# Attention scores in two row halves of the matrix array instead of one product with block-diagonal keys

## The chip, the cores and the metric

The kernel runs on one NeuronCore of one Trainium2 chip. The core has TensorE (PE in the profile; its weight loads are listed apart as PEld), VectorE (DVE), ScalarE (ACT), GpSimd (POOL) and SyncE (SP, which here only issues DMAs). The metric is the device time of one execution in microseconds (us); lower is better.

## What is computed

Attention with keys and values averaged in groups of 8, then two feed-forward layers over the 4608 tokens that come out of it. The part around the change is the first function:

```python
def _attn_ref(q, k, v):                      # each 8 x 8 x 576 x 64: batch, head, token, feature
    B, H, S, D = q.shape
    pool = 8
    Sp = S // pool                           # 72 averaged keys
    scale = 1.0 / np.sqrt(D)
    k_p = k.reshape(B, H, Sp, pool, D).mean(axis=3)
    v_p = v.reshape(B, H, Sp, pool, D).mean(axis=3)
    scores = scale * np.matmul(q, k_p.transpose(0, 1, 3, 2))
    scores = scores - np.max(scores, axis=-1, keepdims=True)
    attn = np.exp(scores)
    attn = attn / (np.sum(attn, axis=-1, keepdims=True) + 1e-09)
    return np.matmul(attn, v_p)

def reference(**kwargs):                     # attn, then 512 -> 2048 -> 512, then 512 -> 1536 -> 512
    x = attn_out.transpose(0, 2, 1, 3).reshape(B * S, H * D)
    x = _moe_ref(x=x, **moe_kwargs)          # g(x @ w_in) @ w_out, g a rational function
    return _moe2_ref(x=x, **moe2_kwargs)     # (sigmoid(x @ w_gate) * (x @ w_val)) @ w_out
```

All of it is in fp32. A head has 64 features, so the sum that makes one score runs over 64 of the array's 128 rows.

## The kernel before

**Tiles and stages.** The tokens are cut into 36 tiles of 128 (`units`). A batch has 576 tokens, four and a half tiles, so four of the tiles hold the end of one batch and the start of the next ("parts"); with them there are 40 parts of a tile. Four tiles make a block of 512 tokens. For each block the attention gives the operand `xs`, and the first feed-forward layer takes 16 steps: `g1` (products into `h`, lines 628 to 630 by the helper `mm3`), the rational function on ACT, DVE and POOL, and `g2` (products into `acc`, the same lines). The attention of a block is woven into the steps of the block before it. The second feed-forward layer has no attention beside it and takes the second half of the time.

**Scores of one part (`tile_attention`, from line 550).** The queries of a tile stand as `raw`: 128 partitions by four groups `j` of 128 tokens, where partitions 0 to 63 hold the features of head 2j and 64 to 127 those of head 2j+1. The averaged keys `kp` have the same two halves. `place_keys` (line 470) copies them, once in a batch, with four ACT instructions (line 476) into `kbd`, a block-diagonal tile that line 733 fills with zeros at the start: the copies put the even head's 72 keys beside zeros in the upper half, the odd head's in the lower half. One matmul (line 569) with a 128-row stationary operand (the queries) and 144 moving columns of `kbd` then gives the scores of two heads. Two such matmuls fill a PSUM bank `sc` with four neighbouring heads, so a part has two PE tasks, each with a bank of its own. DVE takes the maximum (574) and subtracts it (575), ACT the exponential (578), DVE the sum and its reciprocal (583, 584), and POOL the product (586). PE transposes the result (594, `pta`), ACT evacuates it (596, `aT`), and PE multiplies with the averaged values (610, `psx`).

That last product shows in the trace what a divided array does: an even head writes PSUM partitions 0 to 63 and an odd head 64 to 127, so its matmuls run in the two column halves of the array (tile shape "72\*64" in the profile).

**What sets the order.** All tasks up to the last block are handed to a planner (`Planner`, line 49): each has an engine, an estimated cost and a rank, and claims named buffers. The planner runs through estimated time and writes out one fixed order for each engine; the engines then run theirs in that order and wait on semaphores. There are four PSUM banks for `h`, `sc`, `pta` and `psx` beyond the first block, at most three of them for attention and at most three for `h`.

Of the kernel before, what the change touches and what calls it, by code (L numbers as in the profile page):

```python
# [13 lines left out]
AF = mybir.ActivationFunctionType  # L14
ALU = mybir.AluOpType
AX = mybir.AxisListType
# [172 lines left out]
def attention_moe_glu_kernel(ctx: ExitStack, tc: tile.TileContext, q, k, v, w_in, w_out, ca, cb, w_gate, w_val, w_out2, out):  # L189
    nc = tc.nc  # L190

    B, H, S, D = v.shape
# [3 lines left out]
    P = 128  # L196
    POOL = 8
    SP = S // POOL
    NJ = H // 2
# [17 lines left out]
    wp = ctx.enter_context(tc.tile_pool(name="wp", bufs=1))  # L217
# [15 lines left out]
    slots = {"W": [f"w{i}" for i in range(NF1 + FS + NR)], "ST": [f"st{i}" for i in range(6)],  # L233
             "h": [f"b{i}" for i in range(4)], "su": [f"su{i}" for i in range(3)], "y": [f"y{i}" for i in range(3)],
             "m": [f"m{i}" for i in range(3)], "g": [f"g{i}" for i in range(3)], "xs": ["xs0", "xs1"],
             "raw": [f"raw{i}" for i in range(3)], "e": ["e"], "aT": ["aT"], "kp": ["kp"], "vp": ["vp"],
             "vh": ["vh0", "vh1"], "kbd": ["kbd"]}
    slots.update({f"acc{e}": [f"b{4 + e}"] for e in range(NJ)})
    slots.update({n: [n] for n in ("mx0", "mx1", "r0", "r1", "wqt")})
    for n in ("A11", "S2", "S3", "S1", "A12", "A22", "S4"):  # L240
# [4 lines left out]
    pools = {}  # L245
# [204 lines left out]
    def small(shape, name, where, kind=None):  # L450
        return Buf(name, shape, F32, where, kind)

    kbd = small([P, NJ, 2, SP], "kbd", ["kbd"])
    vh, xs, rawq, turned, pooled = {}, {}, {}, [], {}

    def k_cols(c):
# [2 lines left out]
    def keys(b, rank, rank_load):  # L459
# [6 lines left out]
            plan("DVE", dve(m * POOL), rank, lambda raw=raw, m=m, cols=cols: nc.vector.reduce_sum(  # L466
                kp.t[:, cols], raw.t[:, :m * POOL].rearrange("p (s j) -> p s j", j=POOL), axis=AX.X), w=[(kp, c)], r=[raw])
        pooled[b] = kp

    def place_keys(b, rank):  # L470
        kp = pooled.pop(b)
        for js, cs in ((slice(0, NJ // 2), (0, 1, 2)), (slice(NJ // 2, NJ), (2, 3, 4))):
            for e in range(2):
                half = slice(e * D, (e + 1) * D)
                def fn(e=e, js=js, half=half):
                    nc.scalar.activation(kbd.t[half, js, e], kp.t.rearrange("p (j s) -> p j s", s=SP)[half, js], AF.Copy)
                plan("ACT", act(SP * 2), rank, fn,
                    w=[(kbd, (js.start, e))], r=[(kp, c) for c in cs])

    def values0(rank, rank_load):  # L480
        vp = small([P, NCH, D], "vp", ["vp"])
# [68 lines left out]
    def tile_attention(i, rank, gate_on=[]):  # L550
# [8 lines left out]

        for x, (b, n) in enumerate(parts):  # L560
            rows = slice(x * n, (x + 1) * n)
            if i == first[b]:
                place_keys(b, rank)
            for g in range(2):
                sc = psum("sc", own, kind)

                def fn(g=g, sc=sc):
                    for j in (2 * g, 2 * g + 1):
                        nc.tensor.matmul(sc.t[:, (j % 2) * 2 * SP:(j % 2 + 1) * 2 * SP], raw.t[:, j * P:(j + 1) * P], kbd.t[:, j].rearrange("p e s -> p (e s)"), start=True, stop=True)  # L569
                plan("PE", 0.5, rank, fn, w=[sc], r=[raw, (kbd, (2 * g, 0)), (kbd, (2 * g, 1))],  # L570
                     after=(turned[-1:] if blk > 1 else turned[-3:-2]) + gate_on)
                hs = slice(4 * g, 4 * g + 4)
                scv = lambda sc=sc, rows=rows: sc.t[rows, :4 * SP].rearrange("p (h s) -> p h s", s=SP)
                plan("DVE", dve(288) - 0.04, rank, lambda hs=hs, scv=scv, rows=rows: nc.vector.reduce_max(mx.t[rows, hs], scv(), axis=AX.X), w=[(mx, (g, x))], r=[sc])
                plan("DVE", dve(288) - 0.04, rank, lambda hs=hs, scv=scv, rows=rows, n=n: nc.vector.tensor_tensor(
                    out=e_.t[rows, hs, :SP], in0=scv(), in1=mx.t[rows, hs].unsqueeze(2).to_broadcast([n, 4, SP]), op=ALU.subtract),
                    w=[(e_, (g, x))], r=[sc, (mx, (g, x))])
        plan("ACT", act(576), rank, lambda: nc.scalar.activation(e_.t[:, :, :SP], e_.t[:, :, :SP], AF.Exp, scale=scale / POOL),
             w=[(e_, (g, x)) for g in range(2) for x in range(len(parts))])
        r = small([P, H], "r", [f"r{i % 2}"])  # L580
# [148 lines left out]

    T0 = -20.0  # L730
    values_at = {}
    for c in range(1):
        plan("DVE", 0.6, T0, lambda: nc.vector.memset(kbd.t, 0.0), w=[kbd])
    warm = psum("warm", ["acc2"])

    def fn():
        for x in range(12):
            nc.tensor.matmul(warm.t[:, :P], ident, ident, start=True, stop=True)
# [52 lines left out]
    for n in range(N1):  # L791
        i, f = SEQ[n]
        emit_extra(n + 2)
        if n >= SEG and f >= FS:
            wo_stream(f, n - 1.5)
        if n == 3 * SEG + 1:
            half_load(n)
        x = n - last_step
        if x == BX:
            bar = plan("-", 0.0, n, "late", after=[t for t in plan.tasks if any(b.where and b.where[0] in  # L800
                       ("ST", "raw", "e", "aT", "kp", "vp", "vh", "kbd", "mx0", "mx1", "r0", "r1") for b in t.bufs)])
            rawx[0] = Buf("rawx", [P, 8 * TB], F32, ["xs"])
            for h, d, ib, o, m in x_pieces(0):
                load(n, 4 * m / 2, lambda h=h, d=d, ib=ib, o=o, m=m: nc.sync.dma_start(x_dst(h, d, m), x2d[ib].t[:, :, o:o + m]),
                     w=[(rawx[0], (h, d))], r=[x2d[ib]], after=first_mm[-1:])
        if 1 <= x <= NQ:
            t = x - 1
            ring[t] = w_buf("wq")
            src, o = ring_src(t)
            load(n, 512, lambda t=t, src=src, o=o: nc.sync.dma_start(ring[t].t.bitcast(F32), src.t[:, o:o + 2]), w=[ring[t]], r=[src], after=first_mm[-1:])  # L810
        if BX + 3 <= x <= BX + 6:
            for job in X_PREP[x - BX - 3]:
                if job[0] == "split":
# [16 lines left out]
    with tc.manual_schedule():  # L830
# [4 lines left out]
        sm = att.enter_context(tc.tile_pool(name="sm", bufs=1))  # L835
        stage = att.enter_context(tc.tile_pool(name="stage", bufs=1))
        stage_t.append(stage.tile([P, len(slots["ST"]) * 8 * P], F32, name="stage"))
        pools.update(w=wp, b=ps, su=rot, y=rot, m=rot, g=g_p, xs=xs_p, raw=raw_p, e=ap1, aT=ap1, kp=ap1, vp=ap1, vh=ap1, kbd=ap1,
                     mx=sm, r=sm)
        for t in jobs:  # L840
            if t.fn == "late":
# [358 lines left out]
```

## Time and profile before

| what | value |
|---|---|
| median of 3 runs | 1736.67 us (1735.71 to 1737.2) |
| the profiled execution, its own time | 1734.64 us |
| its span, first to last instruction | 1732.6 us |
| mean granted TensorE clock | 0.996 of full speed |
| TensorE busy | 1709.0 us, 99% of the span |
| ScalarE, VectorE, GpSimd busy | 60%, 71%, 42% |

The span is cut into four stretches below: 0 to 32 us (the first block's attention alone), 32 to 110 us (weights come in and are split while the first steps run), 110 to 830 us (steps with attention woven in) and 830 us to the end (no attention). A matmul in fp32 is two records in the profile, each with its weight load; "x8" of line 569 is four matmuls. The durations that the profile gives matmuls overlap, so a cost on PE is read from starts: of the matmul ahead of a group and of the second one after it.

### The profile page before, as it was taken

What the parts mean: (1) busy time and instruction counts of PE and PEld (TensorE: products, weight loads), DVE (VectorE), ACT (ScalarE), POOL (GpSimd) and SP (SyncE); (2) the same over time, 40 slices, a digit from 0 to 9 for tenths busy, and PEclk for the clock granted to TensorE, in tenths of its full rate; (3) what the DMA queues carried; (4) which work ended last, traced back from release to release, by engine and by line L of the source; (5) the groups of instructions that cost most, each with busy time, mean ns of one, the idle gap of its engine ahead of it and who ended that gap; (6) DMA issues with size and microseconds to landing.
All of it is one profiled execution on the core that took longest, in us unless ns stands there. A gap on an engine that the chain in (4) does not pass through costs nothing.

```text
span 1732.6 us, 28635 instructions
## 1 busy us (share of the span) xinstructions
PE 1709.0 (99%) x10044; PEld 1553.5 (90%) x10044; DVE 1235.0 (71%) x2146; ACT 1046.6 (60%) x1957; POOL 730.0 (42%) x807
## 2 busy tenths in 40 slices
PE   7899999999999999999999999999999999999999
PEld 6688888888888888788889999999999999999999
DVE  7898888888887878788786466466466467457456
ACT  6999778787877878898885244244244234235234
POOL 6675356454644646777544320330330330330320
PEclk9999999999999999999999999999999999999999
DMA  7675463545535446775753998888888888888856
GB/s 242 190 278 197 158 192 127 177 145 181 187 116 184 146 157 187 227 239 185 235 181 120 301 317 279 277 265 279 272 272 280 277 265 279 272 270 279 255 181 207
DMA packets 180867, 384.61 MB, mean 222 GB/s; under 512 B 24692, under 2 KB 92276, under 8 KB 180724
## 3 DMA queue, kind: packets, MB, share of 16 engines
q1 hardware_dynamic: 180724, 382.78, 67.4%
q8 instruction: 80, 1.31, 0.3%
q14 instruction: 63, 0.52, 0.1%
HBM read 322.96 MB, written 58.72 MB: 220 GB/s over the span
## 4 chain that ended last, share of the span: by engine, by line
PE 93%; ACT 2%; DMA 1%; DVE 1%; POOL 1%; issue 0%; SPq 0%; POOLq 0%; ACTq 0%
PE h L628 17%; PE h L630 17%; PE h L629 17%; PE acc L628 7%; PE acc L630 7%; PE acc L629 7%; PE acc L1044 5%; PE acc L1043 5%; PE acc L1042 5%; PE sc L569 2%; PE psx L610 2%; PE pta L594 2%; DMA stage<-in_moe_w_in_dram 0%; ACT stage L296 0%; DMA rawv<-in_v_dram 0%
## 5 line engine op out<-in xcount | busy, mean ns | idle before, releaser
L933 DVE TENSOR_TENSOR t<-h,t 128x384 f32<-128x384 f32 x360 | 200.8, 558 | 251.2 <-PE h L630 123.0
L668 POOL TENSOR_TENSOR g<-y,g 128x512 fp32r<-128x512 f32 x143 | 186.6, 1305 | 205.3 <-ACT g L666 175.7
L1002 POOL TENSOR_TENSOR ga<-t 128x384 f32<-128x384 f32 x48 | 48.9, 1019 | 452.5 <-DVE t L933 445.6
L628 PE MATMUL h<-xs,wi 128*128 128x512 f32 x576 | 228.9, 397 | 5.7 <-ACT aT L596 3.6
L628 PE MATMUL acc<-g,wo 128*128 128x512 f32 x576 | 230.1, 399 | 0.0
L630 PE MATMUL acc<-g,wo 128*128 128x512 f32 x576 | 225.2, 391 | 1.9 <-POOL g L668 1.9
L630 PE MATMUL h<-xs,wi 128*128 128x512 f32 x576 | 225.3, 391 | 0.0
L629 PE MATMUL h<-xs,wi 128*128 128x512 f32 x576 | 225.2, 391 | 0.0
L629 PE MATMUL acc<-g,wo 128*128 128x512 f32 x576 | 224.6, 390 | 0.0
L1044 PE MATMUL acc<-wo,go 128*128 128x256 f32 x756 | 213.9, 283 | 0.0
L1043 PE MATMUL acc<-wo,go 128*128 128x256 f32 x756 | 213.9, 283 | 0.0
L1042 PE MATMUL acc<-wo,go 128*128 128x256 f32 x756 | 213.9, 283 | 0.0
L628 PE MATMUL h<-xS,wq 128*128 128x384 f32 x576 | 192.4, 334 | 0.0
L630 PE MATMUL h<-xS,wq 128*128 128x384 f32 x576 | 192.4, 334 | 0.0
L629 PE MATMUL h<-xS,wq 128*128 128x384 f32 x576 | 192.4, 334 | 0.0
L947 ACT ACTIVATE t<-h 128x384 f32<-128x384 f32 x72 | 35.3, 491 | 242.2 <-PE h L630 238.4
L662 DVE SCALAR_TENSOR_TENSOR y<-y,coef,h 128x512 f32<-128x512 f32 x144 | 107.2, 744 | 70.9 <-ACT h L661 70.5
L1044 PEld LDWEIGHTS acc<-wo,go 128*128 128x128 f32 x756 | 145.1, 192 | 0.0
L1043 PEld LDWEIGHTS acc<-wo,go 128*128 128x128 f32 x756 | 145.1, 192 | 0.0
L1042 PEld LDWEIGHTS acc<-wo,go 128*128 128x128 f32 x756 | 145.1, 192 | 0.0
L628 PE MATMUL h<-xA,wq 128*128 128x384 f32 x432 | 144.3, 334 | 0.0
L629 PE MATMUL h<-xA,wq 128*128 128x384 f32 x432 | 144.3, 334 | 0.0
(129 smaller groups left out, 4258.1 us busy)
## 6 DMA issues: line engine op xcount, KB each, us to landing
wq<-w2d SPq DMA_DIRECT2D x252, 512.0 KB
wo<-wo2d SPq DMA_DIRECT2D x126, 512.0 KB
wo<-wod SPq DMA_DIRECT2D x96, 512.0 KB
w2d<-stage SPq DMA_DIRECT2D x36, 512.0 KB
wo2d<-stage SPq DMA_DIRECT2D x84, 128.0 KB
rawk<-in_k_dram SPq DMA_DIRECT2D x32, 256.0 KB
rawq<-in_q_dram SPq DMA_DIRECT2D x32, 256.0 KB
rawv<-in_v_dram SPq DMA_DIRECT2D x32, 256.0 KB
```

Source lines behind the costliest of these rows:

```text
L569: nc.tensor.matmul(sc.t[:, (j % 2) * 2 * SP:(j % 2 + 1) * 2 * SP], raw.t[:, j * P:(j + 1) * P], kbd.t[:, j].rearrange("p e s -> p (e s)"), ...
L628: nc.tensor.matmul(out_, wl, xh, start=start, stop=False, skip_group_check=on)
L629: nc.tensor.matmul(out_, wh, xh, start=False, stop=False, skip_group_check=on)
L630: nc.tensor.matmul(out_, wh, xl, start=False, stop=stop, skip_group_check=on)
L662: plan("DVE", 0.66, rank, lambda: STT(out=y.t, in0=y.t, scalar=coef[:, 0:1], in1=h.t, op0=ALU.add, op1=ALU.mult), w=[y], r=[h])
L668: plan(on, cost, rank, lambda: eng.tensor_tensor(out=g.t[:, 1], in0=y.t, in1=g.t[:, 0].bitcast(F32), op=ALU.subtract), w=[(g, 1)], r=[y, ( ...
L933: nc.vector.tensor_tensor(out=out_, in0=a, in1=b, op=ALU.add)
L947: nc.scalar.activation(t["u"], b[1], AF.Copy)
L1002: eng.tensor_tensor(out=dst, in0=x, in1=y, op=ALU.mult)
L1042: nc.tensor.matmul(a, gh, wh, start=s_ == 0 and not on, stop=False, skip_group_check=on)
L1043: nc.tensor.matmul(a, gh, wl, start=False, stop=False, skip_group_check=on)
L1044: nc.tensor.matmul(a, gl, wh, start=False, stop=s_ == NS - 1, skip_group_check=on)
```

## The change

The block-diagonal tile goes away: its zeroing, its four copies in a batch, and its buffer. The scores of each head become a matmul of their own with a 64-row stationary operand, 128 token columns wide, and 72 moving columns of `kp`. Even heads use rows 0 to 63 of the array and write one bank, odd heads use rows 64 to 127 and write another. A part thus has one PE task of eight matmuls instead of two tasks of two, and claims both banks at once; the planner's cost for it is 0.6 instead of twice 0.5. DVE's two passes over a bank now take heads 0, 2, 4, 6 and heads 1, 3, 5, 7. `kp` gets a second buffer, since matmuls now read it where copies did.

```diff
-             "raw": ..., "e": ["e"], "aT": ["aT"], "kp": ["kp"], "vp": ["vp"],
-             "vh": ["vh0", "vh1"], "kbd": ["kbd"]}
+             "raw": ..., "e": ["e"], "aT": ["aT"], "kp": ["kp0", "kp1"], "vp": ["vp"],
+             "vh": ["vh0", "vh1"]}
...
-    def place_keys(b, rank):
-        kp = pooled.pop(b)
-        for js, cs in ((slice(0, NJ // 2), (0, 1, 2)), (slice(NJ // 2, NJ), (2, 3, 4))):
-            for e in range(2):
-                half = slice(e * D, (e + 1) * D)
-                def fn(e=e, js=js, half=half):
-                    nc.scalar.activation(kbd.t[half, js, e], kp.t.rearrange("p (j s) -> p j s", s=SP)[half, js], AF.Copy)
-                plan("ACT", act(SP * 2), rank, fn, w=[(kbd, (js.start, e))], r=[(kp, c) for c in cs])
...
-            if i == first[b]:
-                place_keys(b, rank)
+            sc = [psum("sc", own, kind) for _ in range(2)]
+
+            def fn(b=b, sc=sc):
+                for j in range(NJ):
+                    for g in range(2):
+                        nc.tensor.matmul(sc[g].t[:, j * SP:(j + 1) * SP], raw.t[g * D:(g + 1) * D, j * P:(j + 1) * P],
+                                         pooled[b].t[g * D:(g + 1) * D, j * SP:(j + 1) * SP], start=True, stop=True)
+            plan("PE", 0.6, rank, fn, w=sc, r=[raw, pooled[b]],
+                 after=(turned[-1:] if blk > 1 else turned[-3:-2]) + gate_on)
             for g in range(2):
-                sc = psum("sc", own, kind)
-
-                def fn(g=g, sc=sc):
-                    for j in (2 * g, 2 * g + 1):
-                        nc.tensor.matmul(sc.t[:, (j % 2) * 2 * SP:(j % 2 + 1) * 2 * SP], raw.t[:, j * P:(j + 1) * P],
-                                         kbd.t[:, j].rearrange("p e s -> p (e s)"), start=True, stop=True)
-                plan("PE", 0.5, rank, fn, w=[sc], r=[raw, (kbd, (2 * g, 0)), (kbd, (2 * g, 1))], ...)
-                hs = slice(4 * g, 4 * g + 4)
+                hs = slice(g, H, 2)
...
-        plan("DVE", 0.6, T0, lambda: nc.vector.memset(kbd.t, 0.0), w=[kbd])
```

New costs and buffers make the planner write another order. Three places matter below.

PE beyond 110 us, at one part's scores (`sc`) between steps of the first layer; the kernel before, a row being one instruction or a run of equal ones:

```order
L629 MATMUL h<-xs,wi_1318 128x512
L630 MATMUL h<-xs,wi_1318 128x512
L569 MATMUL sc<-kbd,rawq 128x144 x4
L628 MATMUL acc_2126<-g,wo_1934 128x512
L629 MATMUL acc_2126<-g,wo_1934 128x512
```

The changed kernel, where the helper's lines are 617 to 619 and the score's is 556:

```order
L618 MATMUL acc_1333<-g,wo_1909 128x512
L619 MATMUL acc_1333<-g,wo_1909 128x512
L556 MATMUL sc<-kp,rawq 128x72 x8
L617 MATMUL h<-xs,wi_1359 128x512
L618 MATMUL h<-xs,wi_1359 128x512
```

Four matmuls of 144 columns became eight of 72, between neighbours that stay matmuls of the whole array. Beyond 110 us there are 31 such parts in both orders, each alone between whole-array matmuls of 512 columns; before, three of the 31 are split into two pieces with other work between them.

SP about 40 us into the program, where the fourth piece of `w_in` (for `stage`) is issued among the copies that spread pooled values (`vh`); the kernel before:

```order
L534 DMA vh<-vp 72x64
L534 DMA vh<-vp 8x64
L534 DMA vh<-vp 64x64
L324 DMA stage<-in_moe_w_in_dram 128x4x256
L544 DMA rawq<-in_q_dram 128x512 x2
```

The changed kernel:

```order
L523 DMA vh<-vp 72x64
L324 DMA stage<-in_moe_w_in_dram 128x4x256
L523 DMA vh<-vp 8x64
L523 DMA vh<-vp 64x64
L533 DMA rawq<-in_q_dram 128x512
```

The weight load moved ahead of the last two of those copies.

ACT about 32 us into the program, at the key copies for the second batch; the kernel before:

```order
L308 ACTIVATE wi1_448<-stage_125 128x512
L296 ACTIVATE stage_125<-stage_125 128x512
L619 ACTIVATE xs_379<-psx_437 128x4x128
L298 ACTIVATE stage_125<-stage_125 128x512
L476 ACTIVATE kbd_126<-kp_331 64x2x72 x4
```

The changed kernel:

```order
L298 ACTIVATE stage_125<-stage_125 128x512
L608 ACTIVATE xs_394<-psx_441 128x4x128
L308 ACTIVATE wi1_460<-stage_125 128x512
L296 ACTIVATE stage_125<-stage_125 128x512
L298 ACTIVATE stage_125<-stage_125 128x512
```

The four copies are gone; ACT goes from one weight piece (`wi1`) to the next conversion (296, 298).

## Rows read from the trace of the kernel before

**Rows 1.** The page's busy times, and its chain that ended last by engine.
```profile
PE 1709.0 (99%) x10044; PEld 1553.5 (90%) x10044; DVE 1235.0 (71%) x2146; ACT 1046.6 (60%) x1957; POOL 730.0 (42%) x807
...
PE 93%; ACT 2%; DMA 1%; DVE 1%; POOL 1%; issue 0%; SPq 0%; POOLq 0%; ACTq 0%
```

**Rows 2.** Busy time by stretch: from:to, length, engines (instructions), granted clock, DMA, GB/s.
```profile
0.00:32.00 32.00, 23.93 (x185) 20.81 (x186) 22.82 (x46) 18.02 (x35) 18.38 (x44) 0.89 0.85 275
32.00:110.00 78.00, 68.26 (x375) 54.91 (x374) 71.02 (x119) 72.01 (x128) 58.55 (x60) 0.96 0.63 205
110.00:830.00 720.00, 717.45 (x3743) 596.38 (x3742) 594.76 (x985) 586.43 (x1052) 410.26 (x487) 1.00 0.54 179
830.00:1732.60 902.60, 899.36 (x5747) 881.41 (x5745) 546.44 (x1000) 370.09 (x746) 242.82 (x219) 1.00 0.78 256
```

**Rows 3.** The score matmuls (line 569) by stretch: PE, PEld, clock, DMA share, GB/s.
```profile
0.00:32.00 32.00, 7.95 (x40) 7.07 (x40) 0.89 0.85 275
32.00:110.00 78.00, 4.70 (x34) 4.44 (x32) 0.96 0.63 205
110.00:830.00 720.00, 35.88 (x248) 34.83 (x248) 1.00 0.54 179
```

**Rows 4.** Timeline of PE: start us, us, instruction; twelve undisturbed steps, then one part's scores.
```profile
87.18 0.39 PE L628 MATMUL acc<-g,wo 128*128 128x512 f32 x1
...
89.90 0.39 PE L628 MATMUL h<-xs,wi 128*128 128x512 f32 x1
...
243.96 0.39 PE L630 MATMUL acc<-g,wo 128*128 128x512 f32 x1
244.19 1.14 PE L569 MATMUL sc<-kbd,rawq 128*128 128x144 f32 x8
...
245.41 0.40 PE L629 MATMUL h<-xs,wi 128*128 128x512 f32 x1
```

**Rows 5.** Timeline of PE at two products with the values, of one and two tiles.
```profile
79.44 0.40 PE L630 MATMUL acc<-g,wo 128*128 128x512 f32 x1
79.77 1.09 PE L610 MATMUL psx<-aT,vh 72*64 72x128 f32 x16
...
81.13 0.39 PE L629 MATMUL acc<-g,wo 128*128 128x512 f32 x1
...
373.92 0.40 PE L630 MATMUL acc<-g,wo 128*128 128x512 f32 x1
...
376.48 0.39 PE L629 MATMUL acc<-g,wo 128*128 128x512 f32 x1
```

**Rows 6.** Weight loads by shape, whole span: busy us, mean ns, idle us before them.
```profile
L630 PEld LDWEIGHTS acc<-g,wo 128*128 128x128 f32 x576 | 108.1, 188 | 26.1 <-POOL g L668 3.3
L610 PEld LDWEIGHTS psx<-aT,vh 72*64 72x64 f32 x384 | 19.1, 137 | 8.1 <-issue 4.7 <-ACT aT L596 1.3 <-ACT h L661 1.1
```

**Rows 7.** Timeline of PEld in the selection of the first batch's values, and its last two loads.
```profile
20.11 0.54 PEld L511 LDWEIGHTS vps<-vp,sel 128*72 128x72 f32 x7
...
21.28 0.41 PEld L511 LDWEIGHTS vps<-vp,sel 128*72 128x72 f32 x3
...
L511 PEld LDWEIGHTS vps<-vp,sel x2: 136/138/139, 21.5 to 21.6; 64*72 64x72 f32 x2
```

**Rows 8.** Timeline of ACT at the four key copies of the second batch.
```profile
31.80 1.33 ACT L476 ACTIVATE kbd<-kp 64x144 f32<-64x144 f32 x4
```

**Rows 9.** Around 40 us: timelines of SP, ACT and PE, and the stretch with the clock.
```profile
37.19 2.09 SPq L534 DMA_DIRECT2D vh<-vp  x3
39.32 0.58 SPq L324 DMA_DIRECT2D stage<-in_moe_w_in_dram  x1
...
43.32 0.67 ACT L296 ACTIVATE stage<-stage 128x512 f32<-128x512 f32 x1 [1.37 <-DMA stage<-in_moe_w_in_dram]
...
45.06 0.80 PE L628 MATMUL h<-xs,wi 128*128 128x512 f32 x1 [2.65 <-ACT aT L596]
...
43.00:50.00 7.00, 4.94 (x12) 3.80 (x12) 5.99 (x11) 6.03 (x11) 2.69 (x3) 0.51 1.02 347
```

More of the change, by code (lines that the diff above doesn't have):

```diff
@@ L235, in attention_moe_glu_kernel @@
              "m": [f"m{i}" for i in range(3)], "g": [f"g{i}" for i in range(3)], "xs": ["xs0", "xs1"],
-             "raw": [f"raw{i}" for i in range(3)], "e": ["e"], "aT": ["aT"], "kp": ["kp"], "vp": ["vp"],
-             "vh": ["vh0", "vh1"], "kbd": ["kbd"]}
+             "raw": [f"raw{i}" for i in range(3)], "e": ["e"], "aT": ["aT"], "kp": ["kp0", "kp1"], "vp": ["vp"],
+             "vh": ["vh0", "vh1"]}
     slots.update({f"acc{e}": [f"b{4 + e}"] for e in range(NJ)})
@@ L451, in small @@
         return Buf(name, shape, F32, where, kind)
-    kbd = small([P, NJ, 2, SP], "kbd", ["kbd"])
     vh, xs, rawq, turned, pooled = {}, {}, {}, [], {}
@@ L468, in keys @@
         pooled[b] = kp
-    def place_keys(b, rank):
-        kp = pooled.pop(b)
-        for js, cs in ((slice(0, NJ // 2), (0, 1, 2)), (slice(NJ // 2, NJ), (2, 3, 4))):
-            for e in range(2):
-                half = slice(e * D, (e + 1) * D)
-                def fn(e=e, js=js, half=half):
-                    nc.scalar.activation(kbd.t[half, js, e], kp.t.rearrange("p (j s) -> p j s", s=SP)[half, js], AF.Copy)
-                plan("ACT", act(SP * 2), rank, fn,
-                    w=[(kbd, (js.start, e))], r=[(kp, c) for c in cs])
     def values0(rank, rank_load):
@@ L561, in tile_attention @@
             rows = slice(x * n, (x + 1) * n)
-            if i == first[b]:
-                place_keys(b, rank)
-            for g in range(2):
-                sc = psum("sc", own, kind)
-                def fn(g=g, sc=sc):
-                    for j in (2 * g, 2 * g + 1):
-                        nc.tensor.matmul(sc.t[:, (j % 2) * 2 * SP:(j % 2 + 1) * 2 * SP], raw.t[:, j * P:(j + 1) * P], kbd.t[:, j].rearrange("p e s -> p (e s)"), start=True, stop=True)
-                plan("PE", 0.5, rank, fn, w=[sc], r=[raw, (kbd, (2 * g, 0)), (kbd, (2 * g, 1))],
-                     after=(turned[-1:] if blk > 1 else turned[-3:-2]) + gate_on)
-                hs = slice(4 * g, 4 * g + 4)
-                scv = lambda sc=sc, rows=rows: sc.t[rows, :4 * SP].rearrange("p (h s) -> p h s", s=SP)
-                plan("DVE", dve(288) - 0.04, rank, lambda hs=hs, scv=scv, rows=rows: nc.vector.reduce_max(mx.t[rows, hs], scv(), axis=AX.X), w=[(mx, (g, x))], r=[sc])
+            sc = [psum("sc", own, kind) for _ in range(2)]
[6 more added lines that the diff above has]
+                 after=(turned[-1:] if blk > 1 else turned[-3:-2]) + gate_on)
+            for g in range(2):
+                hs = slice(g, H, 2)
+                scv = lambda sc=sc[g], rows=rows: sc.t[rows, :4 * SP].rearrange("p (h s) -> p h s", s=SP)
+                plan("DVE", dve(288) - 0.04, rank, lambda hs=hs, scv=scv, rows=rows: nc.vector.reduce_max(mx.t[rows, hs], scv(), axis=AX.X), w=[(mx, (g, x))], r=[sc[g]])
                 plan("DVE", dve(288) - 0.04, rank, lambda hs=hs, scv=scv, rows=rows, n=n: nc.vector.tensor_tensor(
                     out=e_.t[rows, hs, :SP], in0=scv(), in1=mx.t[rows, hs].unsqueeze(2).to_broadcast([n, 4, SP]), op=ALU.subtract),
-                    w=[(e_, (g, x))], r=[sc, (mx, (g, x))])
+                    w=[(e_, (g, x))], r=[sc[g], (mx, (g, x))])
         plan("ACT", act(576), rank, lambda: nc.scalar.activation(e_.t[:, :, :SP], e_.t[:, :, :SP], AF.Exp, scale=scale / POOL),
@@ L731, in attention_moe_glu_kernel @@
     values_at = {}
-    for c in range(1):
-        plan("DVE", 0.6, T0, lambda: nc.vector.memset(kbd.t, 0.0), w=[kbd])
     warm = psum("warm", ["acc2"])
@@ L800, in attention_moe_glu_kernel @@
             bar = plan("-", 0.0, n, "late", after=[t for t in plan.tasks if any(b.where and b.where[0] in
-                       ("ST", "raw", "e", "aT", "kp", "vp", "vh", "kbd", "mx0", "mx1", "r0", "r1") for b in t.bufs)])
+                       ("ST", "raw", "e", "aT", "kp", "vp", "vh", "mx0", "mx1", "r0", "r1") for b in t.bufs)])
             rawx[0] = Buf("rawx", [P, 8 * TB], F32, ["xs"])
@@ L837, in attention_moe_glu_kernel @@
         stage_t.append(stage.tile([P, len(slots["ST"]) * 8 * P], F32, name="stage"))
-        pools.update(w=wp, b=ps, su=rot, y=rot, m=rot, g=g_p, xs=xs_p, raw=raw_p, e=ap1, aT=ap1, kp=ap1, vp=ap1, vh=ap1, kbd=ap1,
+        pools.update(w=wp, b=ps, su=rot, y=rot, m=rot, g=g_p, xs=xs_p, raw=raw_p, e=ap1, aT=ap1, kp=ap1, vp=ap1, vh=ap1,
                      mx=sm, r=sm)
```

## The prediction

> **What bounds the kernel now.** I read the busy times first [rows 1]: PE is busy for 99% of the span and makes 93% of the chain that ended last; the next engine, DVE, stands at 71%. A share over the whole span hides stages, so the stretches come next [rows 2]. PE is idle for 32 - 23.93 = 8.1 us in the first 32 us, for 78 - 68.26 = 9.7 us from 32 to 110 us, for 720 - 717.45 = 2.6 us from there to 830 us and for 3.2 us after. So from 110 us on every nanosecond that PE gains or loses is paid out in full, while DVE (594.76 of 720 us) and ACT (586.43) have about a sixth of that time free. Before 110 us the kernel is held by loads, conversions and waits: from 32 to 110 us ACT and DVE are busy for 72 and 71 of 78 us.
>
> The changed line falls in both regions. The score matmuls show 248 records beyond 110 us [rows 3], eight to a part: 31 parts where PE is the limit. The other nine parts (40 in all) lie in the early stretches.
>
> **What a part's scores cost now.** Whole-array matmuls of 512 columns follow each other at (89.90 - 87.18) / 12 = 0.227 us [rows 4]. Around a part's scores the last of them ahead starts at 243.96 us and the second one behind at 245.41. Without the group two steps would lie between, so 0.454 us go off: 1.45 - 0.454 = 0.99 us. That is 0.124 us for each of eight records, with nothing lost at the group's ends.
>
> **What it will cost: the switch of the array.** The trace holds one kind of work that runs in halves already, the products with the values. One tile of them takes 81.13 - 79.44 - 0.454 = 1.24 us, two take 376.48 - 373.92 - 0.454 = 2.11 us [rows 5]. The second tile thus adds 0.87 us for its 16 records, 0.109 us a pair, and 1.24 - 0.87 = 0.37 us is left over: that is what entering and leaving the halves costs, once for each group. It is no oddity of column halves: at the end of the value selection two matmuls use 64 rows, and around them the loads lag too. Seven loads ahead follow each other at (0.54 - 0.145) / 6 = 0.066 us (0.145 us being the length of one). The row of three loads covers the last whole-height load and the two 64-row ones: its third starts at 21.28 + 0.41 - 0.14 = 21.55 us, two steps in 0.27 us where 0.13 would do [rows 7]. So entering a row half costs 0.14 us; the price of leaving one stands in no row by itself, and I take the 0.37 us for both. The bounds are 0 and 0.4 us. The Trainium skill's page "TensorEngine Tiling (Array Packing)", Key Properties, says that changing the tiling mode drains TensorE; both places of the trace agree.
>
> **What it will cost: the pairs.** Eight matmuls of two records make eight pairs, if an even head runs in the upper rows while an odd one runs in the lower. The column halves do that: 128 moving columns at the score's rate of 0.124 us for 144 would take 0.110 us for each record, and a pair took 0.109. What sets a pair's step here? The moving side shrinks to 72 columns, 0.062 us. The weight load doesn't: the stationary operand still has 128 token columns, on 64 rows instead of 128. Loads of 128 columns last 188 ns, those of 64 columns 137 [rows 6], 0.8 ns a column, so some 0.102 us of a 128-column load grow with its width. In the value selection loads of 72 columns beside only 64 moving ones ran at steps of 0.066 us [rows 7], longer than the 0.055 us for the moving side: there the load sets the step. Scaled from 72 to 128 columns that is between 0.110 (0.8 ns for each further column) and 0.117 us (in proportion). I take 0.112. The least is 0.109, a column pair's step; the most for parallel halves is the 0.124 of today's records. So a part takes 8 x 0.112 + 0.37 = 1.27 us in place of 0.99: 0.28 us more.
>
> The Trainium skill's page "TensorE: Matmul & The Clock Gate", LDWEIGHTS, states the rule that speaks against this change: a load's time follows its columns, whatever the number of rows. By its formula, columns over 1.2, an estimate of a 128-column load is 107 ns, and the part would come out at 8 x 0.107 + 0.37 = 1.23 us; the 188 and 137 ns agree with its slope.
>
> Beyond 110 us: 31 x 0.28 = **+8.6 us**, all of it on the path. With 0.109 and 0.32 us for the switch it would be 31 x 0.2 = 6, with 0.124 and 0.4 it would be 31 x 0.4 = 12.
>
> **The other parts of the change.** The key copies go: four in each of 8 batches, 1.33 us a batch, 10 us of ACT [rows 8]. Beyond 110 us they lie under PE and are worth nothing. The second batch's four, at 31.8 us, stand in the queue of an engine that is nearly full until 110 us, so up to 1.3 us comes back there. The first batch's stand ahead of the first scores, which now wait for the reductions alone. The zeroing on DVE runs before the first keys are in: nothing. DVE's passes keep their number and size.
>
> The order moves the fourth piece of `w_in` ahead of two copies of pooled values on SP. Three such copies take 2.09 us, so it is issued 1.4 us sooner. In the trace it was issued at 39.32 us, ACT's conversion waited for it until 43.32, an evacuation queued behind that, and the matmul at 45.06 us waited 2.65 us; from 43 to 50 us the granted clock was 0.51 of full speed, so mostly at the lower of its two levels (1.2 of 2.4 GHz), with PE idle for long before and in that stretch (4.94 us busy of 7) [rows 9]. A shorter wait gains 1.4 us, and up to 12 x 0.2 = 2.4 us if the clock stays up for the twelve matmuls of that stretch.
>
> Against that, a part now waits for two free banks at once, and DVE can start on the first only when the whole group is nearly done, 0.5 us later than now. Behind it on PE's queue stand the first layer's matmuls; who waits is the maximum, then the exponential, then the transposes. From 110 us on at least 24 whole-array matmuls (5.4 us) stand in the new order between a part's scores and its transposes, so I cost this at nothing there; without that cover it would be 31 x 0.5 = 15 us. The nine early parts pay up to 9 x 0.28 = 2.5 us. Early balance: -1.3 - 1.4 - 0.5 and then + 1.7 for the parts that don't find a wait to hide in: -1.5 us, with -6 and +3 as ends.
>
> **Sum:** +8.6 - 1.5 = +7.1 us. The profiled execution took 1734.64 us, which becomes 1741.7; it lies 2.0 us below the median of 1736.67, so the median goes to **1743.8 us**. Faster or slower by 0.2% (3.5 us) is about what a measurement of this kernel can tell from no change.
>
> **The rivals.**
> (a) *The halves' weight loads follow one another.* Nothing in the trace shows two loads in the two row halves; the column halves' loads do overlap, which speaks against it. Then 16 x 0.112 + 0.37 = 2.16 us a part, 31 x 1.17 = +36 us, and about 1771 us.
> (b) *The other side, the halves run at the moving rate.* If a load hides wholly, a pair takes 0.062 us and a part 8 x 0.062 + 0.37 = 0.87 us: 31 x -0.12 = -3.7, with the early -1.5 about 1731.5 us, faster. It decides from a step below 0.078 us, where a part costs what it does now. The 0.066 us of 72-column loads speaks against it. The Trainium skill's tiling page, Theoretical Speedup, promises up to 2x where a contraction is 64 or less; this is that rule.
> (c) *The switch is free for row halves.* 8 x 0.112 + 0.02 = 0.92 us, 31 x -0.07 = -2.2, with the early stretch 1733 us, on the line between the same and faster. The 0.14 us of [rows 7] speaks against it.
> (d) *The early stretch gives its full 6 us.* +8.6 - 6 = +2.6: 1739.3 us, within 0.2%. For it: 17.8 us of idle PE there; against it: every queue there is full, so one shortened wait mostly uncovers the next.
>
> **How the numbers follow.** Forecast 61%, (a) 13%, (b) 6%, (c) 7%, (d) 13%. The forecast's own range is 1739 to 1751 us; of its 61, some 7 fall below +3.5 us. Slower: 54 + 13 = 67, and 1 of (d): 0.68. Same: 7 + 12 + 3 of (c) = 0.22. Faster: 6 + 4 = 0.10. The range leaves out (a) and (b), 19%, and reaches down to (c): 1732 to 1752.
>
> **What would show it.** Right: the score line with 640 records, its starts in pairs some 0.11 us apart, PE groups of 1.2 to 1.35 us between whole-array matmuls, and beyond 110 us no new wait of PE. Pairs at 0.06 mean (b), single records at 0.11 mean (a), no gap at the ends means (c). The forecast is wrong if new waits on `sc` banks or on DVE's maximum show up on PE, or if the stretch before 110 us ends more than 3 us sooner or later than I put it.

## The result and the profile after

The change makes the kernel slower: 1747.22 us median (1745.50 to 1750.43, six runs) against 1736.40 (1735.13 to 1737.39, six runs) of the kernel before, a ratio of 1.0063 [1.0050, 1.0076]. Run once more on another chip it came to 1748.62 us against 1734.44, 1.0088 [1.0071, 1.0105]. The forecast was 1743.8 us, slower, with a range of 1732 to 1752. So the way was right and the time lies inside the range, and the change costs 11 to 14 us where 7 were forecast. The profiled execution took 1746.89 us, with a span of 1745.1.

The page's busy times and its chain by engine, which answer to [rows 1]:

```profile
PE 1723.7 (99%) x10364; PEld 1554.3 (89%) x10364; DVE 1234.2 (71%) x2145; ACT 1038.0 (59%) x1925; POOL 729.4 (42%) x807
...
PE 90%; ACT 3%; DVE 2%; DMA 2%; POOL 1%; issue 1%; SPq 0%; POOLq 0%; ACTq 0%
```

PE has 320 records more and is 14.7 us longer busy; ACT has lost the 32 key copies and 8.6 us. The chain gives a first hint that longer matmuls are not all of it: 3% of the span went from PE to ACT, DVE and DMA.

The stretches, as in [rows 2] (from:to, length, busy time and instructions of PE, PEld, DVE, ACT, POOL, granted clock, DMA, GB/s):

```profile
0.00:32.00 32.00, 23.95 (x211) 21.42 (x212) 20.66 (x44) 15.94 (x29) 16.94 (x42) 0.79 0.84 274
32.00:110.00 78.00, 72.98 (x422) 58.63 (x422) 64.94 (x116) 70.44 (x121) 57.12 (x61) 0.91 0.61 199
110.00:830.00 720.00, 715.57 (x3942) 583.72 (x3941) 592.72 (x975) 572.98 (x1015) 405.12 (x479) 1.00 0.53 176
```

Beyond 110 us PE is idle for 4.4 us where it was 2.6. In the two early stretches the granted clock is lower than before, 0.79 and 0.91 of full speed in place of 0.89 and 0.96.

The new score line has its 640 matmul records, each with its load. The loads (columns: count, shortest/median/longest ns, first and last start in us, shapes):

```profile
L556 PEld LDWEIGHTS sc<-kp,rawq x640: 182/188/334, 7.5 to 815.4; 64*128 64x128 f32 x160
```

A load of 64 rows and 128 columns takes 188 ns, as long as a load of 128 rows and 128 columns [rows 6]: halving the rows did not shorten it.

PE's timeline around one part (start us, us, instruction, records), to be read as [rows 4] was:

```profile
177.05 0.39 PE L619 MATMUL h<-xs,wi 128*128 128x512 f32 x1
177.37 1.11 PE L556 MATMUL sc<-kp,rawq 64*128 64x72 f32 x16
178.42 0.50 PE L617 MATMUL acc<-g,wo 128*128 128x512 f32 x1
178.75 0.39 PE L618 MATMUL acc<-g,wo 128*128 128x512 f32 x1
```

The part costs 178.75 - 177.05 - 0.454 = 1.25 us, where it cost 0.99. Note the two gaps: the first score starts 0.32 us behind the matmul ahead of it in place of 0.227, and the second whole-array matmul behind the group starts 0.33 us after the first. Record by record the sixteen starts stand 0.007 and 0.105 us apart in turn, so a pair steps by 0.112 us (0.166 from the first pair to the second).

PE's waits from 110 to 840 us (instruction, what it waited for, us in total, times, longest us):

```profile
PE h L617 <- DVE y L653: 2.1, 2, 1.1
PE acc L619 <- POOL g L657: 1.4, 2, 0.8
...
```

The same view of the kernel before:

```profile
PE acc L630 <- POOL g L668: 1.4, 1, 1.4
PE h L628 <- ACT aT L596: 0.9, 1, 0.9
PE h L628 <- DVE y L664: 0.3, 1, 0.3
```

The two waits of 1.1 us on `y`, at 573.2 and 674.7 us, are new; at the first of these places the kernel before waited 0.3 us, at the second not at all. The chain of waits, cut to the time around the first, tells where they come from (start us, us, what):

```profile
568.13 1.09 PE sc L556 x16
569.23 0.80 DVE mx L563 x2
570.03 0.66 DVE y L651
570.69 0.66 DVE u L645
571.35 0.61 DVE h L652
571.95 0.59 DVE y L646
572.54 0.61 DVE y L653
...
573.20 0.50 PE h L617
```

Both banks of a part come ready together, at the end of its one group, and the fixed order of DVE has both maxima there. Five passes of the feed-forward stage stand behind them on DVE, and the next step's matmul `h` needs the last. At this place of the kernel before, the maximum of one bank stood behind the pass that ends in `y`, and the other bank's further back:

```profile
562.70 0.68 DVE L664 SCALAR_TENSOR_TENSOR y<-h,y 128x512 f32<-128x512 f32 x1
...
563.90 0.45 DVE L574 TENSOR_REDUCE mx<-sc 128x4 f32<-128x288 f32 x1
```

The maxima are not all of the wait: experiment 3 has them behind the five passes at the same two steps, and about half of each wait is still there.

### The profile page after: what moved, and what is told of

It is laid out like the page before. It is cut to its first block, busy times and chain, and to the rows that moved or that the text cites. A ratio compares the mean times of both kernels' runs of the same rounds, so it can differ in the third digit from the quotient of the medians.

```text
span 1745.1 us, 29229 instructions
## 1 busy us (share of the span) xinstructions
PE 1723.7 (99%) x10364; PEld 1554.3 (89%) x10364; DVE 1234.2 (71%) x2145; ACT 1038.0 (59%) x1925; POOL 729.4 (42%) x807
## 4 chain that ended last, share of the span: by engine, by line
PE 90%; ACT 3%; DVE 2%; DMA 2%; POOL 1%; issue 1%; SPq 0%; POOLq 0%; ACTq 0%
PE h L617 17%; PE h L618 16%; PE h L619 16%; PE acc L617 7%; PE acc L619 7%; PE acc L618 6%; PE acc L1031 5%; PE acc L1030 5%; PE acc L1029 5%; PE sc L556 2%; PE psx L599 2%; PE pta L583 2%; DMA rawq<-in_q_dram 1%; POOL g L657 1%; ACT y L644 0%
## 5 line engine op out<-in xcount | busy, mean ns | idle before, releaser
L643 ACT ACTIVATE u<-h,coef 128x512 f32<-128x512 f32 x144 | 98.7, 686 | 78.6 <-PE h L619 77.8
L617 PE MATMUL h<-xA,wq 128*128 128x384 f32 x432 | 144.3, 334 | 0.0
```

Source lines behind the costliest of these rows:

```text
L617: nc.tensor.matmul(out_, wl, xh, start=start, stop=False, skip_group_check=on)
L643: ACT(0.57, rank, lambda: nc.scalar.activation(u.t, h.t, AF.Abs, scale=coef[:, 5:6]), w=[u], r=[h, coef_b])
```

## The experiments

**Where the time is lost.** PE runs the same 8748 whole-array matmuls in every kernel here, so the start of the n-th is a clock that compares two kernels at any point of the work. I take the 151st, which ends the early stretches, and the 3301st, behind the last part's scores. Behind that one the kernels run alike, to 0.4 us. In the kernel before, and then in the kernel after, PE's timeline has them at

```profile
91.26 0.39 PE L628 MATMUL h<-xs,wi 128*128 128x512 f32 x1
...
897.48 0.39 PE L628 MATMUL h<-xs,wi 128*128 128x512 f32 x1
```

```profile
92.08 0.39 PE L617 MATMUL h<-xs,wi 128*128 128x512 f32 x1
...
909.62 0.39 PE L617 MATMUL h<-xs,wi 128*128 128x512 f32 x1
```

For six profiles with the new order, read in the same way (the last columns are us behind the kernel before, and how much of that came between the two points):

| kernel | 151st | 3301st | behind, early | behind, 3301st | between |
|---|---|---|---|---|---|
| after | 92.08 | 909.62 | +0.8 | +12.1 | +11.3 |
| after, again | 91.48 | 909.83 | +0.2 | +12.4 | +12.1 |
| new order, whole-array scores | 88.77 | 899.38 | -2.5 | +1.9 | +4.4 |
| halves in the first block alone | 93.40 | 902.82 | +2.1 | +5.3 | +3.2 |
| halves but in the first block | 93.04 | 911.53 | +1.8 | +14.0 | +12.3 |
| halves but in the first block, again | 90.71 | 913.22 | -0.6 | +15.7 | +16.3 |

**1. The new order without the halves.** Everything as in the kernel after, in the same order on every engine, but the eight half-height matmuls become four of the whole array. They read `kp` directly, so each mixes two heads, and the scores are not the attention's.

```diff
-                    for g in range(2):
-                        nc.tensor.matmul(sc[g].t[:, j * SP:(j + 1) * SP], raw.t[g * D:(g + 1) * D, j * P:(j + 1) * P],
-                                         pooled[b].t[g * D:(g + 1) * D, j * SP:(j + 1) * SP], start=True, stop=True)
+                    nc.tensor.matmul(sc[j // 2].t[:, j % 2 * 2 * SP:(j % 2 + 1) * 2 * SP], raw.t[:, j * P:(j + 1) * P],
+                                     pooled[b].t[:, j // 2 * 2 * SP:(j // 2 + 1) * 2 * SP], start=True, stop=True)
```

> The changed kernel's order on every engine, with whole-array score matmuls of the old shape: four of 128 rows and 144 columns a part, on the pooled keys themselves, so the scores mix two heads and the output is not attention; nothing else differs. Theory (the halves cost 0.256 us a part, the rest of the loss is the new order): groups of 0.99 us between whole-array matmuls, 31 x 0.256 = 7.9 us less than the changed kernel, and the waits of PE beyond 110 us stay near the changed kernel's 5 us: 1738 to 1740 us, 2 to 3 us over the kernel before. Rival (the waits come from the longer groups, the order is innocent): the waits fall back to the 2.6 us of before and the time is that of before, 1736 us.

Measured: 1739.03 us median against 1735.06, 1.0021 [1.0012, 1.0030]. The order with the copies gone is not free, and it works both ways: 2.5 us are gained by the 151st matmul, 4.4 lost behind it. Of PE's waits from 90 to 840 us the one on `y` is the kernel after's:

```profile
...
PE h L616 <- DVE y L652: 1.9, 3, 0.9
```

So it is here too, without any halves: 0.9 us in place of 1.1 at the same two places, with a group that is 0.27 us shorter. The rest of the change's cost belongs to the halves: 1746.9 - 1736.6 = 10.3 us between the profiled executions, 6.9 to 7.7 of it between the two points, where 31 x (1.248 - 0.983) = 8.2 us is what the longer groups alone come to.

**2. Only the one task, in the kernel before.** Block-diagonal keys and whole-array scores as before, but one PE task for both banks, with the new cost.

```diff
-            for g in range(2):
-                sc = psum("sc", own, kind)
...
-                    for j in (2 * g, 2 * g + 1):
...
-                plan("PE", 0.5, rank, fn, w=[sc], r=[raw, (kbd, (2 * g, 0)), (kbd, (2 * g, 1))],
+            sc = [psum("sc", own, kind) for _ in range(2)]
...
+                for j in range(NJ):
...
+            plan("PE", 0.6, rank, fn, w=sc, r=[raw] + [(kbd, (g, e)) for g in (0, 2) for e in range(2)],
```

> The kernel before with one edit: a part's scores are one PE task with both banks at the planner's 0.6 us, block-diagonal keys and whole-array matmuls as they were. Theory (claiming both banks at once is harmless beyond 110 us, the halves are what costs): groups of 0.99 us, 1735 to 1739 us. Rival (the two banks make most of the loss): 1742 us or more.

Measured: 1740.24 us, 1.0029 [1.0020, 1.0038], between the two theories. The first of its waits from 60 to 840 us:

```profile
PE h L628 <- DVE y L664: 2.4, 5, 0.9
...
```

The longest of the waits on `y`, 0.9 us, is at the start of the same two steps as in experiment 1 (567.6 and 667.9 us). So one task with the new cost is enough to bring it; neither the halves nor the missing copies are needed. Whether it is the joining or the cost, 0.6 in place of twice 0.5, this edit doesn't tell apart; experiment 3 raises the cost, and a wait on `y` stays at these two steps.

**3. The planner told the true cost.** The one edit to the kernel after is the cost of the task.

```diff
-            plan("PE", 0.6, rank, fn, w=sc, r=[raw, pooled[b]],
+            plan("PE", 1.25, rank, fn, w=sc, r=[raw, pooled[b]],
```

> The changed kernel with the planner's cost of a part's scores raised from 0.6 to the 1.25 us that they take. Theory (the order made with too low a cost lets PE arrive at waits): groups stay 1.25 us, the waits of PE beyond 110 us go from 5 to about 2.5 us and the time to 1744 to 1745 us. Rival (the waits come from claiming two banks at once, or by chance of the order): waits of 3 to 6 us, 1746 to 1748 us.

Measured: 1756.06 us, 1.0115 [1.0099, 1.0130]. Both expectations fell. The truer number gave another order, and a worse one: among PE's waits from 60 to 840 us is one of 1.4 us on an `sc` bank, at 247.95 us, and around it lies a stretch at the lower clock (1.2 of 2.4 GHz); in the 11 us from 236 to 247 us PE had been busy for 9.65.

```profile
...
PE h L617 <- DVE y L653: 1.5, 3, 0.6
PE sc L556 <- DVE xs L609: 1.4, 1, 1.4
...
```

```profile
247.70:254.50 6.80, 6.55 (x25) 5.46 (x26) 4.19 (x9) 1.43 (x3) 6.02 (x11) 0.50 0.37 108
```

The time says nothing on the halves; it says that the order, at the same work, is worth 0.3 to 0.5% (1.0115 against 1.0063 and 1.0088).

This order also prices the maxima at the two steps with the new waits on `y`, since it has them behind the five passes there. DVE around the first of the two:

```profile
577.01 0.75 DVE L651 SCALAR_TENSOR_TENSOR y<-y,coef,h 128x512 f32<-128x512 f32 x1 [0.90 <-ACT h L650]
...
579.57 0.68 DVE L653 SCALAR_TENSOR_TENSOR y<-h,y 128x512 f32<-128x512 f32 x1
...
580.83 0.82 DVE L563 TENSOR_REDUCE mx<-sc 128x4 f32<-128x288 f32 x2
```

The first of the five passes waits 0.90 us for ACT, no maximum stands ahead of it, and PE still waits 0.56 us for `y` at both steps (580.3 and 682.2 us). So some 0.5 of the 1.07 us goes with the maxima, and the rest comes from what feeds the five passes.

**4 and 5. The switch, priced by itself.** One extra whole-array matmul on the identity, two records, is put between the second and the third pair of heads, or ahead of the first. The work is the same; only the first kernel leaves the halves once more.

```diff
+                    if j == 2:
+                        nc.tensor.matmul(sc[1].t[:, 4 * SP:4 * SP + P], ident, ident, start=True, stop=True)
                     for g in range(2):
```

with `j == 0` in the other.

> The changed kernel with one more matmul in each part, identity times identity over the whole array into free columns of the second bank, between the second and the third pair of heads, so the array changes its shape twice more. Theory (each way into the halves and out costs 0.35 us together): a group of 1.25 + 0.22 for the matmul + 0.35 for the second switch = 1.8 us beyond 110 us, 31 x 0.57 = 17 to 18 us over the changed kernel, about 1766 us. Rival (what is left over at a group's ends is the filling of the array, paid once, not a switch): 1.5 us and 1756 us.

> The same extra matmul put ahead of the part's first pair, where whole-array matmuls run anyway: no further change of shape. Theory: 1.25 + 0.22 = 1.47 us a group, some 7 us over the changed kernel, 1754 us, and 0.35 us a group less than with the matmul in the middle. Rival: the same as in the middle.

Measured: 1772.01 us between, 1756.53 us ahead, one run each. PE's timeline of a part, first with the matmul between:

```profile
183.04 0.39 PE L621 MATMUL h<-xs,wi 128*128 128x512 f32 x1
183.36 0.67 PE L558 MATMUL sc<-kp,rawq 64*128 64x72 f32 x8
183.96 0.49 PE L556 MATMUL sc<-ident 128*128 128x128 f32 x2
184.38 0.67 PE L558 MATMUL sc<-kp,rawq 64*128 64x72 f32 x8
184.98 0.50 PE L619 MATMUL acc<-g,wo 128*128 128x512 f32 x1
185.31 0.39 PE L620 MATMUL acc<-g,wo 128*128 128x512 f32 x1
```

and with it ahead:

```profile
179.58 0.39 PE L621 MATMUL h<-xs,wi 128*128 128x512 f32 x1
179.81 0.38 PE L556 MATMUL sc<-ident 128*128 128x128 f32 x2
180.12 1.12 PE L558 MATMUL sc<-kp,rawq 64*128 64x72 f32 x16
181.16 0.50 PE L619 MATMUL acc<-g,wo 128*128 128x512 f32 x1
181.50 0.39 PE L620 MATMUL acc<-g,wo 128*128 128x512 f32 x1
```

Between, the group costs 185.31 - 183.04 - 0.454 = 1.82 us; ahead, 181.50 - 179.58 - 0.454 = 1.47. One visit to the halves and back is thus 0.35 us. The same rows give the pair: sixteen records last 1.12 us and eight 0.67, so four pairs take 0.45 us, 0.112 each. And 8 x 0.112 + 0.35 = 1.25 us is the part. The 15.5 us between the two kernels are more than 40 x 0.35 = 14 by about what one run's scatter is.

**6. One half after the other.** The loop over the halves goes outside, so all upper-row matmuls come before the lower-row ones.

```diff
-                for j in range(NJ):
-                    for g in range(2):
+                for g in range(2):
+                    for j in range(NJ):
```

> The changed kernel with the loops of a part's matmuls turned round: four even heads in the upper rows first, then four odd heads in the lower, so neighbours in the program share a half. Theory (a pair runs at once only when matmuls of the two halves stand next to each other): 16 records at 0.112 us and 0.35 us for the switch, 2.1 us a part, 31 x 0.9 = 28 us more than the changed kernel, about 1775 us. Rival (the engine looks far enough ahead to run the halves beside each other anyway): 1.25 us a part and 1747 us.

Measured: 1767.91 us (one run). The timeline of a part:

```profile
181.91 0.39 PE L619 MATMUL h<-xs,wi 128*128 128x512 f32 x1
182.23 1.62 PE L556 MATMUL sc<-kp,rawq 64*128 64x72 f32 x16
...
184.11 0.39 PE L618 MATMUL acc<-g,wo 128*128 128x512 f32 x1
```

That is 1.75 us, neither the 2.1 of halves that never overlap nor the 1.25 of pairs. The sixteen starts explain it: at both ends of the group they are 0.112 us apart (0.167 from the first to the second); the sixth stands 0.006 us behind the fifth, and the next steps are 0.106, 0.061, 0.050, 0.061, 0.051 and 0.061. The sixth record is the first of the second half: it carries the same wait as the group's first record (in the kernel after the first two records carry it, one of each half), and the first half's closing signal comes with the eleventh start. Records of one half alone step at a load's pace, whatever 72 columns would allow; where the halves meet, some run beside each other, and two take 0.112 us again. So the pairs of the change do overlap, and need to stand close by in the program to do so.

**7. Does the load set the step without halves?** The kernel before with each score matmul cut in two, one head's 72 columns each, with the same 128x128 weights loaded for both.

```diff
-                        nc.tensor.matmul(sc.t[:, (j % 2) * 2 * SP:(j % 2 + 1) * 2 * SP], raw.t[:, j * P:(j + 1) * P], kbd.t[:, j].rearrange("p e s -> p (e s)"), ...)
+                        for e in range(2):
+                            nc.tensor.matmul(sc.t[:, (2 * (j % 2) + e) * SP:(2 * (j % 2) + e + 1) * SP], raw.t[:, j * P:(j + 1) * P], kbd.t[:, j, e], ...)
```

> The kernel before, with its order and its block-diagonal keys, but each score matmul cut in two: 72 columns for one head, the same 128x128 weights loaded for each. No change of array, no order moved. Theory (the load of 128 columns sets the step, whatever the rows it fills and whatever moves behind it): 16 steps of 0.112 us, 1.79 us a part in place of 0.99, so +0.80 x 31 = +25 us: about 1760. Rival (72 moving columns set the step, 0.062 us): 16 x 0.062 = 0.99 us a part and about 1736.

Measured: 1764.61 us (one run). The timeline at a piece of half a part, eight records:

```profile
181.60 0.39 PE L631 MATMUL h<-xs,wi 128*128 128x512 f32 x1
181.83 1.00 PE L570 MATMUL sc<-kbd,rawq 128*128 128x72 f32 x8
...
182.96 0.39 PE L630 MATMUL acc<-g,wo 128*128 128x512 f32 x1
```

It costs 182.96 - 181.60 - 0.454 = 0.91 us, 0.113 for each record, and whole parts of sixteen records cost 1.79. The theory holds: 0.112 us is the step of a 128-column load, of 128 rows here and of 64 in the halves, and the rival's 0.062 us of 72 moving columns shows only once in this group, from its first record to its second (0.061 us); every later step is 0.110 to 0.112 us. Compared with this kernel the halves do what they promise: sixteen records in 0.90 us in place of 1.79, and 0.35 us for the switch.

**8 and 9. Halves in the first block alone, and everywhere else.** Experiment 1 again, with its mixed heads only where `blk > 0`, or only where `blk == 0`.

```diff
+                    if blk > 0:
+                        nc.tensor.matmul(sc[j // 2].t[:, j % 2 * 2 * SP:(j % 2 + 1) * 2 * SP], raw.t[:, j * P:(j + 1) * P],
+                                         pooled[b].t[:, j // 2 * 2 * SP:(j // 2 + 1) * 2 * SP], start=True, stop=True)
+                        continue
                     for g in range(2):
```

> The changed kernel's order with row halves only in the first block's four parts, and whole-array score matmuls (two heads mixed, as in g_same_order, so the output is not attention) in the other 36. Theory (in the first 32 us the halves keep the granted clock at its lower level for longer, 13.7 us in the changed kernel against 3.4 in g_same_order): the clock stays low from about 8.5 us to some 19 or 22 us again, the first whole-array matmul of the first layer starts 1 to 2 us later than in g_same_order and the time is 1 to 3 us over it, 1740 to 1742 us. Rival (that stretch of low clock is chance and has nothing to do with the halves): one dip of 3.4 us, the time of g_same_order, 1739 us.

> The opposite: whole-array score matmuls (mixed heads) in the first block's four parts, row halves in the other 36. Theory: a single short dip of the clock before 32 us, groups of 1.25 us from then on, and 1 to 3 us less than the changed kernel: 1744 to 1746 us. Rival (the clock has nothing to do with the halves): a long dip here too, 1747 us.

Measured: 1740.46 us, 1.0027 [1.0017, 1.0038], and 1752.42 us, 1.0091 [1.0077, 1.0105]. The first block's four groups are worth no more than a measurement can tell (1.0021 without them), though its profiled execution reaches the 151st matmul 4.6 us later than that of experiment 1. The second missed its 1744 to 1746: it seemed slower than the kernel after, which has more halves. So both ran again, side by side.

> The changed kernel once more, beside the kernel with halves in all blocks but the first. That one was 1.0091 of the kernel before and the changed one 1.0063, on different chips, though the first has four halves groups less. If the chip or the run makes the difference, the two come within 2 us of each other here (both 1746 to 1753); if the order of the two does, the changed kernel stays at 1747 and the other at 1752.

> Halves in all blocks but the first, once more (it mixes two heads in the first block, so its scores are not the attention's there). Expected beside the changed kernel: within 2 us of it if the chip or the run makes the difference; 5 us above it if the kernel does.

Measured: 1748.62 us, 1.0088 [1.0071, 1.0105], and 1748.90 us, 1.0081 [1.0067, 1.0096]. They are 0.3 us apart: the 5 us had been the chip and the runs, not the kernel. That also bounds what the table can say: one kernel's two profiled executions differ by 2.3 us at the 151st matmul and by 4 us between the points (the second has a wait of 3.0 us for POOL at 241.6 us and 3.4 us at the lower clock behind it, where the first waits 0.5 us and stays at the higher clock). The 2.5 and 4.4 us of experiment 1 come from one profile and are no surer than that; that its order costs something at all rests on its eleven runs.

**The clock early.** Three kernels in the stretches 12 to 16 and 16 to 22 us (columns as above; the granted clock is the third number from the end). After:

```profile
12.00:16.00 4.00, 3.13 (x22) 2.87 (x23) 3.92 (x10) 0.70 (x2) 3.75 (x6) 0.50 0.94 292
16.00:22.00 6.00, 6.00 (x42) 5.22 (x41) 3.63 (x10) 4.84 (x10) 2.53 (x6) 0.50 0.62 239
```

The same order with whole-array scores (experiment 1):

```profile
12.00:16.00 4.00, 2.47 (x19) 2.29 (x20) 3.93 (x10) 1.27 (x3) 2.99 (x5) 1.00 1.08 342
16.00:22.00 6.00, 5.21 (x59) 4.59 (x59) 5.93 (x15) 5.58 (x14) 3.83 (x8) 1.00 0.71 245
```

The order before with scores of 72 columns (experiment 7):

```profile
12.00:16.00 4.00, 4.00 (x21) 4.00 (x20) 2.44 (x6) 0.99 (x2) 0.79 (x2) 0.50 1.02 329
16.00:22.00 6.00, 6.00 (x30) 5.66 (x30) 4.23 (x11) 2.69 (x5) 4.42 (x8) 0.50 0.55 213
```

With the halves the clock stays at 1.2 GHz through both stretches, and PE gets through 42 instructions in 6 us where it did 59. Experiment 7 does the same without any halves, so a half-height tile is not needed for it; it reaches the 151st matmul at 98.02 us, 6.8 us behind the kernel before. What decides whether the clock comes back at 12 us was not settled: score groups were longer in both kernels, but with halves in the first block alone the clock was low from 10.5 to 20.7 us, and with halves elsewhere alone from 13.5 to 16.9 and from 27.2 to 37.4 us, in its second profile only from 28.1 to 34.9.

## Why the prediction was right, and where its sizes were off

*The pair step* was right: 0.112 us taken, 0.112 measured, and set by the load, as argued from the 188 and 137 ns of [rows 6] and the steps of [rows 7]. Experiment 7 shows the cause and not only the number: the same step at full height. The Trainium skill's page "TensorE: Matmul & The Clock Gate", LDWEIGHTS, gives a load a time by its columns whatever its rows; the trace agrees (188 ns at 64 rows and at 128), and its estimate of 107 ns stands beside steps of 112.

*The switch* was right: 0.37 us read off the column halves of [rows 5], 0.35 us measured for row halves. The Trainium skill's page "TensorEngine Tiling (Array Packing)", Key Properties, has the change of mode drain TensorE; experiments 4 and 5 agree and put a price on it.

*A part's scores* came to 1.25 us in place of 1.27, and 31 x (1.248 - 0.993) = +7.9 us in place of +8.6.

*The rivals on the step fell.* (a), loads one after the other, would have shown 2.16 us a part. (b), the moving rate of 72 columns, would have shown pairs at 0.062 us; it stood beside the up to 2x of the Trainium skill's page "TensorEngine Tiling (Array Packing)", Theoretical Speedup. Experiment 7 agrees with that page against sixteen full-height records (0.90 us for the pairs in place of 1.79); against the block-diagonal product, which brings two heads in one pass at 0.99 us, there is no such gain. (c), a free switch, is excluded by experiments 4 and 5.

*The early balance* was mis-sized. Forecast -1.5 us, measured +0.8 and +0.2 at the 151st matmul, inside the ends of -6 and +3. In experiment 1 the order gained 2.5 us, where the three gains of the sum came to 3.2. Of the gains it named, PE's wait of 2.65 us at 45 us is gone in experiment 1 and in the kernel after. The low clock behind it is not: the granted clock is 0.51 from 43 to 50 us before and from 46 to 53 us after. And in the kernel after the weight piece was issued at 40.29 us, not sooner than the 39.32 of before. What looks too small is the other side: +1.7 us for the longer parts, where the halves took back 2.7 to 3.3 (with the scatter of 2.3 us in mind). The sum reckoned their groups at the full clock; in the profile after they ran at 1.2 GHz for longer. How the 3 us divide between the groups and the clock was not measured apart. Rival (d), the full 6 us, did not come.

*"I cost this at nothing" is the step that failed.* The prediction saw that DVE could start on the first bank only at the end of the group, named the maximum, the exponential and the transposes as those who wait, and found 5.4 us of matmuls as cover. The cover did hold for these three in the profiled execution; in the second one a transpose waited 0.97 us. But DVE's queue holds more than the softmax: behind the maxima stand the five passes that end in `y`, and for those no cover was counted. The chain at 568 us ends in a wait of PE of 1.07 us, and the wait at 674.7 us is as long; some 0.5 us of each goes with the maxima (experiment 3). With the other new waits on ACT and POOL the new order lost 4.4 us between the two points even with whole-array scores (experiment 1), and one task with the new cost brings the waits on `y` by itself (experiment 2). Of the +11.3 us between the points in the kernel after, 7.9 are the groups; the remaining 3.4 are what is left for this term, taken as 0. By the starts of the matmuls some 2.4 of them are PE's waits and the late starts behind them, less those of the kernel before; 1.0 us is spread over steps a little longer than 0.227 us, and its cause stays open. "Beyond 110 us no new wait of PE" was one of the prediction's own signs of being right, and it did not come.

*The sum:* +7.9 for the groups, +0.8 early and +3.4 for waits make +12.1 us at the 3301st matmul; the profiled execution was 1746.89 - 1734.64 = 12.25 us longer than the one before. Forecast were +8.6, -1.5 and 0. That the time still lay inside the range is in part luck: the range had its width from the price of the groups and the early stretch, and nothing in it was meant for waits. The groups came 0.7 us cheaper than forecast, the other two terms 2.3 and 3.4 us dearer.

No version in these runs beats the kernel before. Experiment 3 orders the passes ending in `y` ahead of the maxima at the two steps, halves these waits and is slower all the same, by other waits. An order without any of them was not tried; by the sum above it could win back some 3 us and not the 0.26 us of every part.

## What to carry to other kernels

Splitting an array in halves pays only for what it halves. Before trading zeros in an operand for half-height tiles, look at which of load and moving columns sets the step: here 144 moving columns hid a 128-column load, and 72 no longer could, so the zeros had cost next to nothing, and the switch of 0.35 us a group was a plain loss. And when two tasks become one, ask for each engine that reads the result what else stands behind that read in its queue: a wait that the reader's own chain can hide may be paid by a stranger behind it.

## What the chip showed that was not expected

- Matmuls of the two row halves ran beside each other when the program had four of one half and then four of the other (experiment 6): the second half's first record started 0.006 us behind the fifth of the first half's eight, so ahead of three that stand before it in the program, and up to the end of the first half the steps were 0.05 and 0.06 us in place of 0.112.
- The clock stayed at 1.2 GHz from 12 to 22 us in the kernels with longer first scores, of half height (after) and of full height (experiment 7) alike, while PE was busy for all of the last 6 us; with shorter groups in the same order it was back at 2.4 GHz from 12 us on.
- Orders of the same work, made by the same planner from one changed number, differed by 0.3 to 0.5% of the time (experiment 3), about half of what the edit under study costs.
